# h from fp16 pairs of p and M, and packs of p turned by a transposing DMA instead of by TensorE and ScalarE

## The chip, the cores and the metric

The kernel runs on 1 core of a Trainium2 chip. The metric is the device time in microseconds of one execution. TensorE (PE), VectorE (DVE), ScalarE (ACT), GpSimd (POOL) and SyncE (SP, which issues the transfers here) run side by side and meet at semaphores.

## What is computed

Four batches of 12608 query rows with 128 channels go through an attention over 49 agents; the result goes through a feed-forward layer of 1024 hidden units with a soft gate and a layer norm. Cut to what matters:

```python
def sm(a, b):                      # a softmax of scaled products
    s = scale * (a @ b.transpose(0, 2, 1))
    e = np.exp(s - s.max(-1, keepdims=True))
    return e / (e.sum(-1, keepdims=True) + 1e-09)
agent_v = sm(agents, k) @ v        # 49 x 128 a batch
x = sm(q, agents) @ agent_v        # 12608 x 128 a batch
...
h = x @ w_in                       # 1024 columns
e = np.exp(h - h.max(-1))
solu = h * e / (e.sum(-1) + 1e-09)
ln = (solu - mean) / np.sqrt(var + 1e-06) * g_ln
out = ln @ w_out                   # back to 128 columns
```

## The kernel before

x is never formed. For each batch the kernel makes M = agent_v @ w_in (scaled by the softmax's sum), and then h = p @ M, where p is the softmax of a query over 49 agents. p stands in 128 rows as a pair: the rounded value in rows 0 to 48 and the rest in rows 64 to 112; M stands twice below itself for the same reason, and as a pair of tiles `mh` and `ml` (rounded value and rest), so h is two matmuls for each half of the 1024 columns. All four operands are fp32r, fp32 words that TensorE takes in a rounded form.

The work has three parts:

- **Phase A**, once a batch (`phase_a`): 13 chunks of keys and values, a running softmax of agents over keys, agent_v, then M. `f3` is the product with w_in, `f4h` writes `mh` on ACT, `f4l` writes `ml` on DVE. After that `q1` to `q5` find the largest element of M, turn it into a power of two by way of one row, and spread it to all partitions in `cb`: a scale for u and two constants for the layer norm.
- **Phase B**, once for each unit of 8 tiles of 128 queries (`phase_b`): the products with agents (`b0`), the maximum, the difference, the exponent, the sum, its reciprocal (`b1` to `b3r`), and on POOL the two parts of p, written into one of two standing pack tiles of 4 query tiles each (`b4`). `b5` turns the four 128x128 blocks of a pack on PE (an fp32 transpose against the identity), and `b6` evicts them from PSUM on ACT as `pT`, of which there are `PTB` = 5 buffers.
- **The tiles**, 396 of them: `c_h` makes h in one of two PSUM tensors `ph` of two banks each; `c_max` is the negated row maximum on DVE; `c_exp` the exponent with its sum on ACT; `c_u` is u = h * e times the scale, with its sum, on DVE; `c_sq` the sum of squares on ACT. For the last product u must have its 1024 columns on the partitions. `xbar(x)` chooses how: tiles with x % PEN in PEP (1 of 4, and the last two) are turned by PE in fp32 (`c_t`) and evicted by ACT (`c_ev`), and take 8 fp32 matmuls with w_out; the others are split into an fp16 pair (`c_f0` on POOL or ACT, `c_f1` on POOL), turned by a transposing DMA from SP's queue (`c_x`), and take 24 fp16 matmuls. Both are `c_w`. `c_rstd` and `c_fin` scale the result, `c_out` stores it for 4 tiles at a time.

The order of the work on each engine is fixed when the kernel is built. The class `Plan` keeps a clock for each engine; each operation has a cost, a due time and the operations that it depends on, and the plan picks for each engine what can start soonest, by the earliest due. Four PSUM banks (`px`) are handed out in the same way. The due times come from some 70 constants (`BD0` to `AEND`) that shift each kind of operation against its tile's number. What the plan says is no time of the chip: there each engine runs its list in this order and waits on semaphores.

The names that the steps touch are on lines 586 to 631 and 688 to 704 (M and its scale), 762 to 812 (p), 816 to 864 (tiles) and 985 to 1033 (what waits for what).

Of the kernel before, what the change touches and what calls it, by code (L numbers as in the profile page):

```python
# [9 lines left out]
F32 = mybir.dt.float32  # L10
# [125 lines left out]
def kernel(  # L136
# [15 lines left out]
    P = 128  # L152
# [9 lines left out]
    CPR = 792.07  # L162
    PEP = (1,)
    PEN = 4
# [4 lines left out]
    FBUF = 4  # L169
# [7 lines left out]
    BD0 = -86.23  # L177
    BD1 = -476.94
    BD2 = 170.01
    BD3 = -515.84  # L180
    BD4 = -91.39
    BD5 = -179.77
    DH = -885.13
    DMX = 874.48
    DEX = -1050.28
    DU_ = -614.84
    DSQ = 160.15
    DT = -700.62
    DEV = -791.75
    DLD = -174.95  # L190
    DW = -64.88
    DWF = 612.88
    DHF = 174.12
    DMXF = 238.03
    DEXF = -551.41
    DUF = -1018.36
    DSQF = 695.01
    AME = -96.53
    ANM = 44.67
    AEE = 89.07  # L200
    ATT = 88.11
    AET = -637.77
    AAC = -693.49
    DR = 253.95
    DFG = -705.01
    DF_ = -71.98
    DRP = 262.68
    DF0 = 954.83
    DF1 = -831.63
    DX = -85.44  # L210
    OUTD = -880.66
    OUTC = 693.15
# [6 lines left out]
    SHY = -127.74  # L219
    DHR = 489.74  # L220
    DHL = -776.94
    DMXR = 1618.01
    DMXL = -140.03
    DEXR = 898.58
    DEXL = -83.71
    DUR = -1207.82
    DUL = -701.04
    DSQR = -395.96
    DSQL = -416.83
    DTR = 489.84  # L230
    DTL = 1240.02
    DEVR = -656.35
    DEVL = 605.88
    DLDR = 445.47
    DLDL = 347.94
    DWR = -351.47
    DWL = 192.65
    ASP = 0.85
    MZ = 276.64
    ASTART = 110.74  # L240
    AEND = -395.53
# [86 lines left out]
    def load_out():  # L328
        nc.sync.dma_start(out=g_sb, in_=g_ln)
        for h in range(2):  # L330
            wd = words["out", h] = mpool.tile([P, HW, 2], I32, tag="mh" if h == 0 else "ml", name=f"wd_out{h}")
            nc.sync.dma_start(out=wd.rearrange("p (k d) t -> p k (d t)", d=C),
                              in_=wo[h * (DF // 2) : (h + 1) * (DF // 2), :].rearrange("(k p) d -> p k d", p=P))
# [86 lines left out]
    for i in range(2):  # L420
        nc.vector.tensor_tensor(out=fold[:, i, :], in0=ident[:, :AP2], in1=ident[:, AP2:], op=ALU.add)
    av_dup = const.tile([C, 2 * AP2], F32, name="av_dup")
# [12 lines left out]
    def phase_a(b, due, gate):  # L435
# [155 lines left out]
        def f4h(hf):  # L591
# [3 lines left out]
            pmm, rs, mh = ps["w", hf], res["rs"], bmats[b]["mh"]  # L595
            nc.scalar.mul(out=mh[:, sl], in_=pmm, mul=rs)

        def q1():
            res["pk"] = tiny.tile([P, 1], F32, tag="pk", bufs=2, name=f"pk{b}")
            nc.vector.tensor_reduce(out=res["pk"], in_=bmats[b]["mh"].bitcast(F32), op=ALU.max, axis=AX.X,  # L600
                                    apply_absolute_value=True)

        def q2(px):
            ps["q"] = px
            nc.tensor.transpose(px[:1, :P], res["pk"], ident)

        def q3():

            r = res["pr"] = tiny.tile([1, 2], F32, tag="pr", bufs=2, name=f"pr{b}")
            ri = r.bitcast(I32)  # L610
            nc.vector.tensor_reduce(out=r[:, 0:1], in_=ps.pop("q")[:1, :P], op=ALU.max, axis=AX.X)
            nc.vector.tensor_scalar(out=r[:, 1:2], in0=r[:, 0:1], scalar1=1e-30, scalar2=None, op0=ALU.max)
            nc.vector.tensor_scalar(out=ri[:, 0:1], in0=ri[:, 1:2], scalar1=0x7F800000, scalar2=0x7F800000,
                                    op0=ALU.bitwise_and, op1=ALU.bitwise_xor)

        def q4(px):
            ps["q"] = px
            nc.tensor.matmul(px[:, :1], ones[:1, :], res["pr"][:, :1], start=True, stop=True)

        def q5():  # L620
            cb = cbs[b] = bpool.tile([P, 3], F32, tag="cb", name=f"cb{b}")
            px = ps.pop("q")
            for i, k in enumerate((1.0, math.sqrt(1e-6 * DF) * DF, math.sqrt(1e-6 * DF) * DF * 1e-9)):
                nc.vector.tensor_scalar(out=cb[:, i : i + 1], in0=px[:, :1], scalar1=float(2.0 ** 13), scalar2=k,
                                        op0=ALU.mult, op1=ALU.mult)

        def f4l(hf):
            sl = slice(hf * HW, (hf + 1) * HW)
            pmm, rs, mh, ml = ps.pop(("w", hf)), res["rs"], bmats[b]["mh"], bmats[b]["ml"]
            nc.vector.scalar_tensor_tensor(out=ml[:, sl], in0=pmm, scalar=rs, in1=mh[:, sl].bitcast(F32),  # L630
                                           op0=ALU.mult, op1=ALU.subtract)
# [71 lines left out]
        CB[b] = op("D", q5, 0.36, at(z), [o], free=o)
# [23 lines left out]
    def phase_b(k, dues, gate=()):  # L727
# [34 lines left out]
        def b3r():  # L762
            nc.vector.reciprocal(out=r["s"], in_=r["s"])

        def b4(q):
# [5 lines left out]
            nc.gpsimd.tensor_scalar(out=pk[:, :m, :A].bitcast(F32R), in0=dv, scalar1=1.0, scalar2=0.0,  # L771
                                    op0=ALU.mult, op1=ALU.add)
            nc.gpsimd.tensor_tensor(out=pk[:, :m, AP2 : AP2 + A].bitcast(F32R), in0=dv, in1=pk[:, :m, :A],
                                    op=ALU.subtract)

        def b5(q, px):
            m = min(GT, nt - q * GT)
            r["pt", q] = px
            for j in range(m):
                nc.tensor.transpose(px[:, j * P : (j + 1) * P], packs[q][:, j, :], ident)  # L780

        def b6(q):
            m = min(GT, nt - q * GT)
            pT = pTs[b, t0 // GT + q] = bpool.tile([P, GT * P], F32R, tag="pT", bufs=PTB, name=f"pT{b}_{t0}_{q}")
            nc.scalar.copy(out=pT[:, : m * P], in_=r.pop(("pt", q))[:, : m * P])
# [15 lines left out]
        d5 = op("D", b3r, 0.12, dues[3] + 0.2, [d3])  # L801
        for q in range(nq):
# [13 lines left out]
    def c_h(x, hf):  # L816
# [3 lines left out]
        lhs = pTs[b, g][:, j * P : (j + 1) * P]  # L820
# [4 lines left out]
    def c_max(x):  # L825
        nms[x] = tiny.tile([P, 1], F32, tag="nm", name=f"nm{x}")
        nc.vector.tensor_reduce(out=nms[x], in_=phs[x], op=ALU.max, axis=AX.X, negate=True)  # L827

    def c_exp(x):
# [4 lines left out]
        nc.scalar.activation(out=es[x], in_=phs[x], func=AF.Exp, bias=nms[x], accum_out=rs_[R]["S"][:, j : j + 1])  # L834
# [4 lines left out]
    def c_u(x):  # L839
        us[x] = (epool.tile([P, DF], F32, tag="u", bufs=UBUF, name=f"u{x}"), tiny.tile([P, 1], F32, tag="su", name=f"su{x}"))  # L840
        u, su = us[x]
        nc.vector.scalar_tensor_tensor(out=u, in0=phs[x], scalar=cbs[seq[x][0]][:, :1], in1=es[x],  # L842
# [142 lines left out]
    for x in range(n):  # L985
# [7 lines left out]
        for hf in range(2):  # L993
            H[x, hf] = op("P", F(c_h, x, hf), 0.468, at(x, DH + (0.0 if xbar(x) else DHF), DHR, DHL) + 0.02 * hf,
                          [pT_op[b, t // GT], U.get(x - 2)] + mdone[b][: hf + 1], kind=0)
        grp_h[b, t // GT] = last_h[b] = H[x, 1]
        MX[x] = op("D", F(c_max, x), 1.14, at(x, DMX + (0.0 if xbar(x) else DMXF), DMXR, DMXL), [H[x, 0], H[x, 1]])
        EX[x] = op("A", F(c_exp, x), 1.115, at(x, DEX + (0.0 if xbar(x) else DEXF), DEXR, DEXL), [MX[x], U.get(x - 2), FIN.get((x // RT - 4) * RT // GT + RT // GT - 1)] + (cout if x < 2 else []), after=[EX.get(x - 1)])
        used = [T.get((x - UBUF, 0)), T.get((x - UBUF, 1)), SQ.get(x - UBUF), F1.get(x - UBUF)]
        U[x] = op("D", F(c_u, x), 1.215, at(x, DU_ + (0.0 if xbar(x) else DUF), DUR, DUL), [EX[x], CB[b]] + used, after=[U.get(x - 1)])  # L1000
        SQ[x] = op("A", F(c_sq, x), 1.185, at(x, DSQ + (0.0 if xbar(x) else DSQF), DSQR, DSQL), [U[x]] + ([om] if not x else []))
        if xbar(x):
# [3 lines left out]
                       [U[x], old] + ([] if old else wready if (len(fl) + 2) % FBUF == 2 else cin + cout),  # L1006
# [100 lines left out]
```

## Time and profile before

| what | value |
|---|---|
| median of 3 runs | 1341.16 us (1340.59 to 1342.35) |
| the profiled execution | 1340.84 us, of which the span of its instructions is 1339.1 |
| mean granted TensorE clock | 0.997 |
| DMA | 262.66 MB in 653547 packets, mean 196 GB/s |
| transposing DMAs of xt | 295, of 16 blocks of 128x128 each |

The span runs from the first to the last instruction. An engine's busy time is the union of its instructions' durations. Matmuls overlap in the pipeline, so what one costs is read from the start of one to the start of the next, and the same holds on DVE, where an instruction starts before the one ahead has ended. "Idle before, releaser" names what ended the idle time. In the groups, L823 is the line of h, L827 the row maximum, L842 u, L834 the exponent, L863 the squares, L891 the last product, L870 the transposes of u on PE, L875 their eviction, L780 and L785 those of p, L853 and L850 the fp16 parts of u on POOL, L857 the transposing DMA.

### The profile page before, as it was taken

The page shows a single profiled execution, that of the slowest core. Times are in us where ns is not written, and L with a number is a line of the kernel's source. Part 1 is how long each engine was busy: PE and PEld are TensorE (multiplying, and loading weights), DVE is VectorE, ACT ScalarE, POOL GpSimd, SP SyncE. Part 2 cuts the span into 40 slices and gives each one's busy share as a digit, 9 for nine tenths or more (in the row PEclk, how much of TensorE's full clock was granted, in tenths as well). Part 3 has the DMA queues.
Part 4 walks back from the last instruction along what each step waited for, and adds up shares of the span by engine and source line. Part 5 has one row for each costly group of instructions (what it writes and reads, how often), then busy time and mean ns, then how long its engine had stood idle before and what let it go on. Part 6 is the DMA issues. An engine that isn't in the chain of part 4 may idle for free.

```text
span 1339.1 us, 36596 instructions
## 1 busy us (share of the span) xinstructions
PE 1310.8 (98%) x14406; PEld 1127.5 (84%) x14406; DVE 1208.5 (90%) x1807; ACT 1223.3 (91%) x2258; POOL 1166.7 (87%) x1160
## 2 busy tenths in 40 slices
PE   8889999999999999999999999999899999999998
PEld 4568888888998888888888888988788888988988
DVE  6898899999998899999999999998889899999885
ACT  3489899899999999999999999999898999999996
POOL 2569899899998999998899999997689999999995
PEclk9989999999999999999999999999999999999999
DMA  9569999989989999999999999999789999987987
GB/s 363 216 153 200 247 216 238 199 171 193 177 159 223 216 190 237 218 237 191 188 186 180 212 224 197 191 239 177 155 153 186 179 182 185 170 171 143 178 165 139
DMA packets 653547, 262.66 MB, mean 196 GB/s; under 512 B 618560, under 2 KB 622144, under 8 KB 653376
## 3 DMA queue, kind: packets, MB, share of 16 engines
q1 hardware_dynamic: 653376, 260.34, 94.1%
q8 instruction: 113, 1.85, 0.6%
q14 instruction: 58, 0.48, 0.1%
HBM read 79.67 MB, written 25.95 MB: 79 GB/s over the span
## 4 chain that ended last, share of the span: by engine, by line
PE 79%; ACT 7%; DVE 6%; POOL 3%; DMA 3%; issue 2%; SPq 0%; ACTq 0%; DVEq 0%; POOLq 0%
PE px L891 37%; PE ph L823 24%; PE px L870 6%; PE px L740 3%; PE px L780 3%; ACT e L834 2%; PE px L476 2%; ACT sq L863 2%; PE px L525 2%; DMA xt<-f 2%; DVE u L842 1%; POOL f L853 1%; PE px L509 1%; DVE nm L827 1%; ACT ut L875 1%
## 5 line engine op out<-in xcount | busy, mean ns | idle before, releaser
L853 POOL TENSOR_TENSOR f<-u,f 128x1024 f16<-128x1024 f32 x295 | 631.1, 2144 | 38.2 <-ACT f L848 16.7
L842 DVE SCALAR_TENSOR_TENSOR u<-ph,cb,e 128x1024 f32<-128x1024 f32 x396 | 500.0, 1280 | 40.1 <-ACT e L834 34.5
L827 DVE TENSOR_REDUCE nm<-ph 128x1 f32<-128x1024 f32 x396 | 477.4, 1217 | 45.8 <-PE ph L823 40.4
L863 ACT ACTIVATE sq<-u,su 128x1024 bf16<-128x1024 f32 x396 | 457.4, 1155 | 23.3 <-DVE u L842 18.4
L834 ACT ACTIVATE e<-ph,nm 128x1024 f32<-128x1024 f32 x396 | 439.5, 1112 | 24.2 <-DVE nm L827 21.4
L891 PEld LDWEIGHTS <-xt 128*128 128x128 f16 x7080 | 404.7, 98 | 47.5 <-issue 43.3
L891 PE MATMUL px<-wh,xt 128*128 128x128 f16 x4720 | 441.2, 220 | 1.5 <-DMA xt<-f 1.5
L891 PE MATMUL px<-wl,xt 128*128 128x128 f16 x2360 | 409.3, 219 | 0.0
L823 PE MATMUL ph<-mh,pT 128*128 128x512 f32 x792 | 344.2, 435 | 4.5 <-DVE u L842 4.5
L823 PE MATMUL ph<-ml,pT 128*128 128x512 f32 x792 | 312.8, 395 | 0.0
L850 POOL TENSOR_SCALAR f<-u 128x1024 f16<-128x1024 f32 x234 | 244.5, 1045 | 33.2 <-DVE u L842 20.1
L891 PE MATMUL px<-w,ut 128*128 128x128 f32 x1616 | 215.9, 278 | 0.6 <-DVE ob L935 0.6
L891 PEld LDWEIGHTS px<-w,ut 128*128 128x128 f32 x1616 | 197.8, 192 | 10.9 <-issue 6.8
L823 PEld LDWEIGHTS ph<-mh,pT 128*128 128x128 f32 x792 | 150.0, 189 | 37.7 <-DVE u L842 11.3
L823 PEld LDWEIGHTS ph<-ml,pT 128*128 128x128 f32 x792 | 150.7, 190 | 19.5 <-issue 0.7
L875 ACT COPY ut<-px 128x512 f32<-128x512 f32 x202 | 114.4, 582 | 6.6 <-PE px L870 6.5
L870 PE MATMUL px<-ident,u 128*128 128x128 f32 x808 | 110.5, 274 | 0.0
L870 PEld LDWEIGHTS px<-ident,u 128*128 128x128 f32 x808 | 95.3, 142 | 13.4 <-ACT ek L502 0.2
L914 POOL TENSOR_TENSOR y<-t,nhalf 128x8 f32<-128x8 f32 (+1 forms) x50 | 81.4, 1628 | 3.8
L935 DVE TENSOR_TENSOR ob<-px,yc 128x512 f32<-128x512 f32 (+1 forms) x100 | 68.0, 680 | 13.7 <-PE px L891 9.3
L834 ACT ACTIVATION_READ_ACCUMULATOR e<-ph,nm 128x1 f32 x396 | 79.1, 200 | 0.0
L863 ACT ACTIVATION_READ_ACCUMULATOR sq<-u,su 128x1 f32 x396 | 77.5, 196 | 0.0
(133 smaller groups left out, 1219.4 us busy)
## 6 DMA issues: line engine op xcount, KB each, us to landing
out_dram<-ob SPq DMA_DIRECT2D x98, 256.0 KB, 3.0
qt<-in_qT_dram SPq DMA_DIRECT2D x48, 512.0 KB, 4.8
kt<-in_kT_dram SPq DMA_DIRECT2D x36, 512.0 KB, 4.8
vt<-in_v_dram SPq DMA_DIRECT2D x36, 512.0 KB, 5.1
kh<-in_kT_dram SPq DMA_DIRECT2D x12, 512.0 KB, 9.9
vh<-in_v_dram SPq DMA_DIRECT2D x12, 512.0 KB, 10.0
xt<-f SPq DMA_TRANSPOSE x295, 4.8
wd_in<-in_w_in_dram SPq DMA_DIRECT2D x2, 512.0 KB, 6.1
```

Of the source, the lines that this page charges most:

```text
L823: nc.tensor.matmul(ph[:, sl], lhs, bmats[b]["mh" if m == 0 else "ml"][:, sl], start=(m == 0), stop=(m == 1))
L827: nc.vector.tensor_reduce(out=nms[x], in_=phs[x], op=ALU.max, axis=AX.X, negate=True)
L834: nc.scalar.activation(out=es[x], in_=phs[x], func=AF.Exp, bias=nms[x], accum_out=rs_[R]["S"][:, j : j + 1])
L842: nc.vector.scalar_tensor_tensor(out=u, in0=phs[x], scalar=cbs[seq[x][0]][:, :1], in1=es[x], op0=ALU.mult, op1=ALU.mult, accum_out=su)
L850: nc.gpsimd.tensor_scalar(out=f[:, 0, :], in0=us[x][0], scalar1=1.0, scalar2=0.0, op0=ALU.mult, op1=ALU.add)
L853: nc.gpsimd.tensor_tensor(out=fs[x][:, 1, :], in0=us[x][0], in1=fs[x][:, 0, :], op=ALU.subtract)
L863: nc.scalar.activation(out=sq, in_=u, func=AF.Square, bias=su, scale=-float(DF), accum_out=rs_[R]["Q"][:, j : j + 1])
L870: nc.tensor.transpose(pt[:, kf * P : (kf + 1) * P], us[x][0][:, k0 * P : (k0 + 1) * P], ident)
L875: (nc.scalar.copy if k == "A" else nc.vector.tensor_copy)(out=pr[x][:, 4 * hf : 4 * hf + 4, :], in_=rr[x, hf].rearrange("p (k t) -> p k t" ...
L891: nc.tensor.matmul(po, ut, wt[:, kf, :], start=(q == 0), stop=(q == len(mm) - 1))
L914: gp.tensor_tensor(out=g("y"), in0=g("t"), in1=nhalf[:, :m], op=ALU.pow)
L935: nc.vector.tensor_tensor(out=obs[G][:, j0:j1], in0=st[G]["po"].rearrange("p (j d) -> p j d", d=C)[:, j0:j1], in1=rs_[G * GT // RT]["yc"][ ...
```

## The change

- p is scaled by 2^10 and written as an fp16 pair; M is scaled by a power of two, found from its own size, and written as an fp16 pair. So h comes out scaled, and every reader of `ph` undoes that: the row maximum becomes a minimum of h times a negative scale from `cb`, with an accumulator and a tile `junk` that nobody reads; exp gets a scale from `cb` beside its bias; u needs its scale no longer.
- The scale of M must therefore be known before M is written: `q1` (now over the two halves in PSUM), `q1m`, `q2` to `q6` stand between the product and `f4h`, and the row maximum waits for `CB` where u did.
- The pack of p is turned by a transposing DMA from SBUF on SP's queue straight into `pT`; the transposes on PE, their PSUM bank and the eviction on ACT go.
- 3 of 10 tiles go over PE, in place of 1 of 4.
- `FBUF` is 5 in place of 4, the words of w_out are loaded into `fpool`, some costs of the plan and all its due times are new.

The core of the diff (due times and costs of the plan left out):

```diff
-    PEP = (1,)
-    PEN = 4
+    PS = 10
+    PEP = (1, 4, 7)
+    PEN = 10
-    FBUF = 4
+    FBUF = 5
...
-        pk = const.tile([P, GT, P], F32, name=f"pack{i}")
+        pk = const.tile([P, GT, P], F16, name=f"pack{i}")
...
+        def q1(hf):
+            if hf == 0:
+                res["pk"] = tiny.tile([P, 2], F32, tag="pk", bufs=2, name=f"pk{b}")
+            nc.vector.tensor_reduce(out=res["pk"][:, hf : hf + 1], in_=ps["w", hf], op=ALU.max, axis=AX.X,
+                                    apply_absolute_value=True)
+        def q1m():
+            nc.vector.tensor_scalar(out=res["pk"], in0=res["pk"], scalar1=res["rs"], scalar2=None, op0=ALU.mult)
...
-                bmats[b] = {m: mpool.tile([P, DF], F32R, tag=m, name=f"{m}{b}") for m in ("mh", "ml")}
+                bmats[b] = {m: mpool.tile([P, DF], F16, tag=m, name=f"{m}{b}") for m in ("mh", "ml")}
...
-            nc.scalar.mul(out=mh[:, sl], in_=pmm, mul=rs)
+            nc.scalar.mul(out=bmats[b]["mh"][:, sl], in_=ps["w", hf], mul=cbs[b][:, 0:1])
...
             nc.vector.reciprocal(out=r["s"], in_=r["s"])
+            nc.vector.tensor_scalar(out=r["s"], in0=r["s"], scalar1=float(2.0 ** PS), scalar2=None, op0=ALU.mult)
...
-        def b5(q, px):
-            for j in range(m):
-                nc.tensor.transpose(px[:, j * P : (j + 1) * P], packs[q][:, j, :], ident)
-        def b6(q):
-            nc.scalar.copy(out=pT[:, : m * P], in_=r.pop(("pt", q))[:, : m * P])
+        def b5(q):
+            pT = pTs[b, t0 // GT + q] = bpool.tile([P, GT, P], F16, tag="pT", bufs=PTB, name=f"pT{b}_{t0}_{q}")
+            nc.sync.dma_start_transpose(out=pT[:, :m, :], in_=packs[q][:, :m, :].rearrange("p j a -> p (j a)"))
...
-        nc.vector.tensor_reduce(out=nms[x], in_=phs[x], op=ALU.max, axis=AX.X, negate=True)
+        nc.vector.tensor_scalar(out=junk, in0=phs[x], scalar1=cbs[seq[x][0]][:, 3:4], scalar2=None, op0=ALU.mult, op1=ALU.min,
+                                accum_out=nms[x])
...
-        nc.scalar.activation(out=es[x], in_=phs[x], func=AF.Exp, bias=nms[x], accum_out=rs_[R]["S"][:, j : j + 1])
+        nc.scalar.activation(out=es[x], in_=phs[x], func=AF.Exp, bias=nms[x], scale=cbs[seq[x][0]][:, 4:5], accum_out=rs_[R]["S"][:, j : j + 1])
...
-        nc.vector.scalar_tensor_tensor(out=u, in0=phs[x], scalar=cbs[seq[x][0]][:, :1], in1=es[x],
+        nc.vector.scalar_tensor_tensor(out=u, in0=phs[x], scalar=1.0, in1=es[x],
                                        op0=ALU.mult, op1=ALU.mult, accum_out=su)
...
-        MX[x] = op("D", F(c_max, x), ..., [H[x, 0], H[x, 1]])
+        MX[x] = op("D", F(c_max, x), ..., [H[x, 0], H[x, 1], CB[b]])
-        U[x] = op("D", F(c_u, x), ..., [EX[x], CB[b]] + used, after=[U.get(x - 1)])
+        U[x] = op("D", F(c_u, x), ..., [EX[x]] + used, after=[U.get(x - 1)])
```

More of the change, by code (lines that the diff above doesn't have):

```diff
@@ L175 @@
     WC = 4
[L177 to L212, printed above, removed]
+    BD0 = 513.34
+    BD1 = -77.12
+    BD2 = 94.62
+    BD3 = -717.88
+    BD4 = -309.91
+    BD5 = 228.66
+    DH = -1256.09
+    DMX = 581.29
+    DEX = -1973.58
+    DU_ = -1008.76
+    DSQ = -72.06
+    DT = -1102.95
+    DEV = -976.43
+    DLD = -427.49
+    DW = -195.51
+    DWF = 855.88
+    DHF = -429.63
+    DMXF = 612.41
+    DEXF = 162.23
+    DUF = -718.92
+    DSQF = 1579.43
+    AME = 387.52
+    ANM = 375.78
+    AEE = -726.91
+    ATT = -405.51
+    AET = -210.77
+    AAC = -597.68
+    DR = 328.58
+    DFG = 478.21
+    DF_ = -71.82
+    DRP = -396.35
+    DF0 = 1557.5
+    DF1 = 112.95
+    DX = -99.26
+    OUTD = 233.27
+    OUTC = 944.92
     VA = 7
@@ L330, in load_out @@
         for h in range(2):
[L331 removed]
+            wd = words["out", h] = fpool.tile([P, HW, 2], I32, tag="f", name=f"wd_out{h}")
             nc.sync.dma_start(out=wd.rearrange("p (k d) t -> p k (d t)", d=C),
@@ new lines, in q2, with q3 @@
+        def q2(px):
+            ps["q"] = px
+            for i in range(2):
+                nc.tensor.transpose(px[:1, i * P : (i + 1) * P], res["pk"][:, i : i + 1], ident)
+        def q3():
+            r = res["pr"] = tiny.tile([1, 4], F32, tag="pr", bufs=2, name=f"pr{b}")
+            ri = r.bitcast(I32)
+            nc.vector.tensor_reduce(out=r[:, 3:4], in_=ps.pop("q")[:1, : 2 * P], op=ALU.max, axis=AX.X)
+            nc.vector.tensor_scalar(out=r[:, 2:3], in0=r[:, 3:4], scalar1=1e-30, scalar2=None, op0=ALU.max)
+            nc.vector.tensor_scalar(out=ri[:, 1:2], in0=ri[:, 2:3], scalar1=0x7F800000, scalar2=None, op0=ALU.bitwise_and)
+            nc.vector.tensor_scalar(out=ri[:, 0:1], in0=ri[:, 1:2], scalar1=0x7F800000, scalar2=None, op0=ALU.bitwise_xor)
@@ new lines, in q4, with q5, q6 @@
+        def q4(px):
+            ps["q"] = px
+            nc.tensor.matmul(px[:, :2], ones[:1, :], res["pr"][:, :2], start=True, stop=True)
+        def q5():
+            cb = cbs[b] = bpool.tile([P, 5], F32, tag="cb", name=f"cb{b}")
+            px = ps["q"]
+            nc.vector.tensor_scalar(out=cb[:, 0:1], in0=px[:, 0:1], scalar1=res["rs"], scalar2=float(2.0 ** (13 - PS)),
+                                    op0=ALU.mult, op1=ALU.mult)
+        def q6():
+            cb, px = cbs[b], ps.pop("q")
+            for i, j, k in ((1, 0, math.sqrt(1e-6 * DF) * DF), (2, 0, math.sqrt(1e-6 * DF) * DF * 1e-9)):
+                nc.vector.tensor_scalar(out=cb[:, i : i + 1], in0=px[:, j : j + 1], scalar1=float(2.0 ** 13), scalar2=k,
+                                        op0=ALU.mult, op1=ALU.mult)
+            for i, k in ((3, -(2.0 ** -14)), (4, 2.0 ** -14)):
+                nc.vector.tensor_scalar(out=cb[:, i : i + 1], in0=px[:, 1:2], scalar1=k, scalar2=None, op0=ALU.mult)
@@ L603, in q2 @@
[L603 to L625, printed above, removed]
+            nc.scalar.mul(out=bmats[b]["mh"][:, sl], in_=ps["w", hf], mul=cbs[b][:, 0:1])
```

107 lines of the change are left out of this document (51 added, 56 removed).

## The prediction

> **What bounds the kernel now.** I read the page's first part, then the chain that ended last, the busy time by stage, the waits, and for prices the timeline of one stretch and the groups of instructions.
>
> ```profile
> span 1339.1 us, 36596 instructions
> PE 1310.8 (98%) x14406; PEld 1127.5 (84%) x14406; DVE 1208.5 (90%) x1807; ACT 1223.3 (91%) x2258; POOL 1166.7 (87%) x1160
> ```
>
> The chain, by engine and by line:
>
> ```profile
> PE 79%; ACT 7%; DVE 6%; POOL 3%; DMA 3%; issue 2%; SPq 0%; ACTq 0%; DVEq 0%; POOLq 0%
> PE px L891 37%; PE ph L823 24%; PE px L870 6%; PE px L740 3%; PE px L780 3%; ACT e L834 2%; PE px L476 2%; ACT sq L863 2%; PE px L525 2%; DMA xt<-f 2%; DVE u L842 1%; POOL f L853 1%; PE px L509 1%; DVE nm L827 1%; ACT ut L875 1%
> ```
>
> TensorE is the bound: 79% of the chain. The next view has, for three stages, the length and then the busy time (and count) of PE, weight loads, DVE, ACT and POOL.
>
> ```profile
> 0.00:100.00 100.00, 84.16 (x774) 55.68 (x775) 81.35 (x172) 53.03 (x113) 48.30 (x64) 0.97 0.74 243
> 100.00:1250.00 1150.00, 1141.74 (x12708) 994.92 (x12707) 1059.03 (x1548) 1094.64 (x2014) 1045.54 (x1031) 1.00 0.97 195
> 1250.00:1339.00 89.00, 84.90 (x928) 76.90 (x927) 68.15 (x89) 75.61 (x133) 72.91 (x67) 1.00 0.86 159
> ```
>
> (The last three columns are the granted clock, the DMA share, which counts a packet's waiting too, and GB/s.) In the middle 1150 us PE holds 99.3%, but ACT already 95.2%, DVE 92.1%, POOL 90.9%. So a gain on PE is worth its full size only until the next engine is full. DVE's longest waits are for PE's h and for ACT's exponent:
>
> ```profile
> DVE nm L827 <- PE ph L823: 40.4, 99, 1.5
> DVE u L842 <- ACT e L834: 34.5, 77, 2.8
> ```
>
> **The change, term by term.** First PE, from starts of neighbouring matmuls (start, duration, line), since their durations overlap.
>
> ```profile
> 500.62 0.22 PE L891 MATMUL px<-wh,xt 128*128 128x128 f16 x1
> 500.65 0.48 PE L823 MATMUL ph<-mh,pT 128*128 128x512 f32 x1
> 500.97 0.39 PE L823 MATMUL ph<-ml,pT 128*128 128x512 f32 x1
> ...
> 505.29 0.39 PE L823 MATMUL ph<-ml,pT 128*128 128x512 f32 x1
> ...
> 506.92 1.04 PE L870 MATMUL px<-ident,u 128*128 128x128 f32 x8
> 507.79 0.61 PE L891 MATMUL px<-w,ut 128*128 128x128 f32 x4
> 508.24 0.22 PE L891 MATMUL px<-wh,xt 128*128 128x128 f16 x1
> ...
> 508.46 0.22 PE L891 MATMUL px<-wl,xt 128*128 128x128 f16 x1
> ```
>
> 1. *h in fp16.* Seven h matmuls run from 505.29 to 506.92: 0.233 us each. Four fp16 ones of 128 columns take 0.22 us (508.24 to 508.46, the second to fourth left out). So 512 columns in fp16 cost between 0.22 and 0.233 (no faster than now). I take 0.22, the row of the same type: 4 x 396 x 0.013 = 21 us off, 0 at worst. Going from an fp16 run into h, the first h matmul takes 0.32 (500.65 to 500.97) and the fp16 one before it 0.03 instead of 0.055: 0.06 us that fp16 h should not have. At one such entry for every second or third tile (an estimate from this stretch) that is 9 us (0 to 12). The Trainium skill (TensorE: Matmul & The Clock Gate, Back-to-back issue gap) gives N / 2.4 + 2.5 ns, so 216 ns here; the trace's 128-column step agrees, no row has 512 columns in fp16, and by 216 ns the 21 us would be 27.
>
> 2. *Packs of p not turned on PE.* Eight fp32 transposes take 0.87 us (506.92 to 507.79), 0.109 each. 396 go: 43 us off.
>
> 3. *Tiles.* 1 of 4 over PE becomes 3 of 10: 295 tiles over the DMA become 276, so 19 more go over PE. Each adds 8 x 0.109 of transposes and 8 x 0.1125 (507.79 to 508.24, four) and drops 24 x 0.055: 1.77 - 1.32 = 0.45 us, 9 us on.
>
> PE in all: -21 - 9 - 43 + 9 = -64 us (-35 without any gain in h). One execution took 1340.84 us here, 1.7 over its span and 0.3 under the median 1341.16. PE alone would allow 1340.8 - 64 = 1277.
>
> Now the others.
>
> ```profile
> L780 PE MATMUL px<-ident,pack 128*128 128x128 f32 x396 | 59.7, 275 | 3.6 <-ACT ut L875 3.4
> L785 ACT CAST pT<-px 128x512 fp32r<-128x512 f32 x96 | 55.4, 581 | 3.6 <-PE px L780 3.6
> ...
> L875 ACT COPY ut<-px 128x512 f32<-128x512 f32 x202 | 114.4, 582 | 6.6 <-PE px L870 6.5
> ...
> L853 POOL TENSOR_TENSOR f<-u,f 128x1024 f16<-128x1024 f32 x295 | 631.1, 2144 | 38.2 <-ACT f L848 16.7
> ```
>
> 4. *ACT* loses the evictions of p (55 us, and four shorter ones: some 57) and gains 38 of u (38 x 0.582 = 22). exp gets its scale from a pointer beside its bias. Nearest rows, small activations with both pointers and with the bias alone:
>
> ```profile
> L906 ACT ACTIVATE t<-S,cb 128x8 f32<-128x8 f32 x46 | 18.1, 393 | 0.0
> L556 ACT ACTIVATE facp<-nmp,gm 128x13 f32<-128x13 f32 x4 | 1.3, 323 | 0.1
> ```
>
> 393 - 323 = 70 ns at most, 28 us over 396; at least nothing. Those two apply different functions, so I take half, 14. ACT: -57 + 22 + 14 = -21 (-35 to -7). *POOL* drops 19 residues of 2.144, 41 us, and some first halves; the planner may pass it a few casts of ACT.
>
> 5. *DVE.* The row maximum becomes a scaled minimum with an accumulator and a pointer; u loses its pointer.
>
> ```profile
> 504.50 1.28 DVE L842 SCALAR_TENSOR_TENSOR u<-ph,cb,e 128x1024 f32<-128x1024 f32 x1
> 505.70 0.08 DVE L842 DVE_READ_ACCUMULATOR u<-ph,cb,e 128x1 f32 x1
> 505.70 0.69 DVE L481 TENSOR_REDUCE mxp<-px 128x1 f32<-128x512 f32 x1
> 506.31 1.22 DVE L827 TENSOR_REDUCE nm<-ph 128x1 f32<-128x1024 f32 x1
> 507.44 0.20 DVE L488 TENSOR_SCALAR nmp<-mxp,nmp 128x1 f32<-128x1 f32 x1
> ```
>
> Two groups that differ in one pointer operand (busy us, mean ns):
>
> ```profile
> L488 DVE TENSOR_SCALAR nmp<-mxp,nmp 128x1 f32<-128x1 f32 x48 | 10.0, 207 | 0.2
> ...
> L486 DVE TENSOR_SCALAR nmp<-mxp 128x1 f32<-128x1 f32 x4 | 0.6, 150 | 0.0
> ```
>
> From start to start the maximum takes 1.13, and u, with PSUM source, pointer and accumulator, 1.20; its accumulator read hides beside the next instruction (both start at 505.70). So the new minimum costs 0 to 0.07 more; I take 0.07, since u is the same kind: 28 us on. A pointer costs 207 - 150 = 57 ns, if all of that is seen from start to start: 0 to 23 us off u; I take 23. The second small instruction after the reciprocal, 52 x 0.15, adds 8. The chain that finds the scale of M (two half maxima of 0.61 for one of 1.13 and some five small ones of 0.15 to 0.2) adds about 1 us in each of four batches, 4. DVE: +28 - 23 + 8 + 4 = +17 (-11 to +40).
>
> 6. *M now waits for its scale*, and the maximum waits for that chain instead of u. In the head of the chain of waits:
>
> ```profile
> 60.05 1.09 PE px L589 x2
> ...
> 70.71 1.21 DVE u L842 x2
> ```
>
> M's product ends at 61.1, but u starts at 70.7 because the scale came late. The new order, by rows: half maximum 0.69, three steps on one row and two on PE (about 2.5 with gaps), M and its rest 1.5, h 0.9, minimum and exp 2.4: u at about 69. I count nothing; up to 4 us if other DVE work stands in between. In the later batches PE has the tiles of the batch before as cover; without it 3 x 3.5 = 10 us.
>
> 7. *SP's queue.* 100 transposes of p join it, waiting for POOL's pack. Behind such a wait stand xt's transposes, loads and stores; the last matmuls wait for xt.
>
> ```profile
> L857 SPq DMA_TRANSPOSE xt<-f x295: 1317/2403/6232, 75.3 to 1321.9; - x148
> ...
> DMA to landing us min/median/max: 4.2/4.8/9.2
> ```
>
> The stores and loads issued, and how long two of them held SP:
>
> ```profile
> out_dram<-ob SPq DMA_DIRECT2D x98, 256.0 KB, 3.0
> qt<-in_qT_dram SPq DMA_DIRECT2D x48, 512.0 KB, 4.8
> kt<-in_kT_dram SPq DMA_DIRECT2D x36, 512.0 KB, 4.8
> vt<-in_v_dram SPq DMA_DIRECT2D x36, 512.0 KB, 5.1
> ```
>
> ```profile
> 1008.65 0.99 SPq L939 DMA_DIRECT2D out_dram<-ob  x1
> ...
> 1011.52 0.34 SPq L720 DMA_DIRECT2D qt<-in_qT_dram  x1
> ```
>
> xt moves 16 blocks and holds SP 1.3 to 6.2 us, 2.4 in the median: 709 us. After: 276 x 2.4 = 663, and p's quarter size at 0.6 (0.3 to 6.2, were size no matter) another 60, so SP carries 14 us more. The landing's median is close to its least, so the queue isn't full now, and five buffers of p let it run groups ahead. I price this at nothing; uncovered it is 4.2 to 9.2 us a group. The Trainium skill (VectorE: DVE Perf Modes, Rules for kernel authors) speaks against the step: a 128x128 transpose belongs on TensorE if PSUM will do, and its table has 1309 ns by DMA. The rows disagree for a batch of blocks: 4.2 / 16 = 0.26 us each, landing included.
>
> **Sum.** DVE's middle stage becomes 1059 + 17 x 0.91 = 1075 us of work, against PE's 1142 - 64 x 0.91 = 1084. So PE and DVE are nearly level, PE the fuller by 9 us, each leaning on the other through two h buffers, with ACT at 1075 behind unless casts move to POOL. Level engines won't all reach PE's present 99.3%; today's second engine holds 95.2%. I take 97% for DVE, between the two: 1075 / 0.97 = 1108, in which PE's 1084 are 98%. With head and tail of 100 + 89 and 1.7 outside the span: **1299 us**.
>
> **Rivals.**
> - *PE stays the bound and DVE follows without stalls* (minimum costs no more than the maximum did): the full 64 us, 1277; for it, PE reaches 99.3% beside an ACT at 95%. Chance 0.21.
> - *fp16 h is no faster than now* and the mode entries stay: PE gives 35 us, 1306, and with stalls of 10 us 1316. For it: no row has the shape. Chance 0.14.
> - *Slower: DVE becomes the bound and stays as full as today.* h, minimum, exp and u of a tile follow each other on two buffers, with a longer minimum in the loop; if DVE keeps 92.1% there and has its upper cost, (1059 + 36) / 0.921 = 1189, so 1380. It decides from a share of 1075 / 1150 = 93.5% down. Against it: 75 of DVE's idle us are waits for PE and for ACT, which both get lighter. Chance 0.10.
> - *The queue becomes the bound.* Each p transposed holds SP h us: 663 + the 218 stores and loads quoted, at 0.34 to 0.99 and so about 0.65 (142) + 100 h. At the median 2.4 that is 1045 and hidden; at the longest 6.2, 1425. It passes 1341 from h = 5.4. By the skill's 1309 ns a block (VectorE: DVE Perf Modes, The three transpose paths) h would be 4 x 1.309 = 5.2 and the queue's work 1329. The trace's 0.26 us a block speaks against that. Chance 0.05.
>
> **Numbers.** Forecast case 0.50, rivals 0.21, 0.14, 0.10 and 0.05. Differences within 0.2% (2.7 us) can't be told from none. The first three cases are faster: 0.85, and 0.01 of the queue, 0.86; same 0.03; slower 0.11. The range runs from the first rival, less 3 for mode entries at 12 us and 2 for a head in which u starts at 69, 1272, to the third case with DVE's upper cost, 1075 + 21 at 97%, 1130 + 191 and 10 us of stalls: 1331.
>
> **What would show it.** Right: no L780 and L785 groups; h steps of 0.22; DVE's share in the middle near 97%, PE's near 98%; nm's group near 1280 ns with an accumulator read, u's near 1220; few waits for pT. Wrong: PE still at 99% (first rival); h steps of 0.233 (second); DVE at 93% with longer waits for ph or e (third); weight loads of h, or matmuls on xt, waiting for a DMA (fourth).

## The result, and the profile after

The changed kernel takes 1485.14 us (median of 4 runs, 1483.28 to 1486.94), the kernel before beside it 1341.76 (4 runs, 1340.59 to 1344.23). The ratio is 1.1066, with a 95% interval of 1.1042 to 1.109: 143 us slower, where 1299 us had been forecast with a range of 1272 to 1331.

The page's first part for the changed kernel, busy time and share of the span by engine:

```profile
span 1484.7 us, 36533 instructions
PE 1322.9 (89%) x14049; PEld 1028.4 (69%) x14049; DVE 1265.1 (85%) x2275; ACT 1240.9 (84%) x2201; POOL 1096.3 (74%) x1117
```

No engine is full. Beside the page of before, every share has fallen: PE from 98 to 89%, ACT from 91 to 84, POOL from 87 to 74. The chain that ended last is followed back only to 758 us of the span; its line by engine:

```profile
ACT 13%; DVE 12%; POOL 8%; PE 7%; issue 5%; DMA 3%; SPq 0%; DVEq 0%; POOLq 0%; ACTq 0%
```

These shares are of the whole span and sum to 48%. Of the first half the chain says nothing, and in the second no engine leads. So the waits have to be read. Five rows of the view of waits (engine and tile, what ended the wait, us in total, times, longest; "issue" means that the view names nothing that ended it):

```profile
POOL pack L788 <- DMA pT<-pack: 227.8, 54, 9.3
PEld L833 <- issue: 126.3, 181, 6.7
PE ph L833 <- DVE u L853: 77.4, 64, 6.6
ACT e L845 <- DVE junk L837: 66.7, 67, 7.2
...
DVE logits L768 <- POOL pack L790: 43.7, 14, 6.2
```

The longest is new. Before POOL writes p into a pack, it waits for the DMA that still has to read the same tile's last content: 54 times, 4.2 us on average. Before the change the same wait was for PE's transposes, and cost next to nothing; the row in the waits of before:

```profile
POOL pack L771 <- PE px L780: 5.4, 11, 1.3
```

One such wait in the changed kernel, from the timelines of SP and POOL put in order of time (start, duration; on SP the duration is how long the transfer held the engine):

```profile
491.13 0.55 POOL L790 TENSOR_TENSOR pack<-logits,pack 128x196 f16<-128x196 f32 x1
...
507.68 7.71 SPq L868 DMA_TRANSPOSE xt<-f  x3
514.06 4.22 POOL L864 TENSOR_TENSOR f<-u,f 128x1024 f16<-128x1024 f32 x2
515.49 0.53 SPq L950 DMA_DIRECT2D out_dram<-ob  x1
516.22 3.31 SPq L868 DMA_TRANSPOSE xt<-f  x1
518.23 0.52 POOL L786 TENSOR_TENSOR logits<-logits,sm 128x196 f32<-128x196 f32 x1
519.62 0.53 SPq L458 DMA_DIRECT2D kt<-in_kT_dram  x1
520.24 1.20 SPq L796 DMA_TRANSPOSE pT<-pack  x1
524.95 0.36 POOL L788 TENSOR_SCALAR pack<-logits 128x196 f16<-128x196 f32 x1 [6.20 <-DMA pT<-pack]
```

The pack of line 491.13 is turned by the DMA of 520.24. That DMA has its place in SP's list behind the four xt transposes, the store and the load that are shown, and SP starts it as soon as the load ahead is off. The xt transposes in turn wait for POOL's `f`: that of 516.22 starts when the first of the two residues of 514.06 is done (2.11 us each, so at 516.17). POOL works until 518.75, comes to the next pack for the same tile, and stands still for 6.20 us until the DMA has landed. Everything behind on POOL stands too, the next `f` among it, and with it the next xt. So the two lists take turns in holding each other up.

Over all 100 packs, the DMA is issued 20.9 us after the write of its pack has ended, and has landed after 24.4 (medians, from the trace). With 1.0 for the write, a round through a pack takes 25.4 us. Packs are written 13.4 us apart, so two of them leave 26.8. Before the change the turn on PE started as late, 21.0 us after the write, but was over 0.6 us later: a round of 22.6 out of 26.4. So hardly anything is left to spare now, and in 54 rounds it isn't enough.

How long these transfers take (hold of SP in ns, min/median/max; then issue to landing in us), from the view of the tile `pT`:

```profile
L796 SPq DMA_TRANSPOSE pT<-pack x100: 1190/1218/2471, 41.2 to 1425.6; - x100
...
DMA to landing us min/median/max: 2.3/3.2/8.3
```

By stage (length, busy PE, weight loads, DVE, ACT, POOL, granted clock, DMA share, GB/s):

```profile
100.00:1190.00 1090.00, 961.28 (x10173) 746.97 (x10171) 922.47 (x1658) 921.16 (x1635) 798.63 (x811) 0.95 0.88 177
1190.00:1485.00 295.00, 280.00 (x3139) 230.85 (x3137) 261.59 (x437) 273.25 (x470) 253.51 (x248) 1.00 0.88 164
```

Up to 1190 us POOL is at 73% and PE at 88%, and PE's granted clock is 0.95. The last pack wait ends at 1183 (50 of the 54 lie before 970; the last load of keys and values, which share SP's queue, starts at 1044). After that all engines are fuller, and the clock is 1.00.

The groups that answer to those of before (busy us, mean ns), with instructions of different shapes kept apart:

```profile
L837 DVE TENSOR_SCALAR_CACHE_REDUCE junk<-ph,cb 128x1024 bf16<-128x1024 f32 x396 | 506.6, 1279 | 51.1 <-PE ph L833 34.9
L853 DVE SCALAR_TENSOR_TENSOR u<-ph,e 128x1024 f32<-128x1024 f32 x396 | 478.9, 1220 | 72.5 <-ACT e L845 34.9 <-POOL f L864 30.6 <-POOL t L922 2.4
L845 ACT ACTIVATE e<-ph,nm,cb 128x1024 f32<-128x1024 f32 x396 | 475.6, 1203 | 70.4 <-DVE junk L837 66.7
...
L780 DVE TENSOR_SCALAR sm<-sm 128x8 f32<-128x8 f32 x48 | 34.9, 727 | 1.6
```

The minimum (L837) and u (L853) have the lengths that the prediction gave them. The exponent has grown from 1112 to 1203 ns, and the small factor 2^10 on the sums (L780) takes 727 ns where 150 were counted.

### The profile page after: what moved, and what is told of

Same layout as the page of the kernel before. It is cut to its first block, busy times and chain, and to the rows that moved or that the text cites. A ratio compares the mean times of both kernels' runs of the same rounds, so it can differ in the third digit from the quotient of the medians.

```text
span 1484.7 us, 36533 instructions
## 1 busy us (share of the span) xinstructions
PE 1322.9 (89%) x14049; PEld 1028.4 (69%) x14049; DVE 1265.1 (85%) x2275; ACT 1240.9 (84%) x2201; POOL 1096.3 (74%) x1117
## 5 line engine op out<-in xcount | busy, mean ns | idle before, releaser
L864 POOL TENSOR_TENSOR f<-u,f 128x1024 f16<-128x1024 f32 x276 | 587.8, 2136 | 51.0 <-ACT f L859 28.8
L837 DVE TENSOR_SCALAR_CACHE_REDUCE junk<-ph,cb 128x1024 bf16<-128x1024 f32 x396 | 506.6, 1279 | 51.1 <-PE ph L833 34.9
L853 DVE SCALAR_TENSOR_TENSOR u<-ph,e 128x1024 f32<-128x1024 f32 x396 | 478.9, 1220 | 72.5 <-ACT e L845 34.9
L845 ACT ACTIVATE e<-ph,nm,cb 128x1024 f32<-128x1024 f32 x396 | 475.6, 1203 | 70.4 <-DVE junk L837 66.7
L833 PE MATMUL ph<-mh,pT 128*128 128x512 f16 x792 | 308.6, 390 | 80.3 <-DVE u L853 77.4
L833 PE MATMUL ph<-ml,pT 128*128 128x512 f16 x792 | 308.2, 389 | 0.0
L833 PEld LDWEIGHTS <-pT 128*128 128x128 f16 x1584 | 149.7, 99 | 225.6 <-issue 126.3
L902 PE MATMUL px<-w,ut 128*128 128x128 f32 x1920 | 253.7, 279 | 1.2 <-DVE ob L946 1.2
L902 PEld LDWEIGHTS px<-w,ut 128*128 128x128 f32 x1920 | 236.7, 193 | 20.9 <-issue 10.9
L845 ACT ACTIVATION_READ_ACCUMULATOR e<-ph,nm,cb 128x1 f32 x396 | 77.7, 196 | 0.0
```

Source lines behind the costliest of these rows:

```text
L833: nc.tensor.matmul(ph[:, sl], lhs, bmats[b]["mh" if m == 0 else "ml"][:, sl], start=(m == 0), stop=(m == 1))
L837: nc.vector.tensor_scalar(out=junk, in0=phs[x], scalar1=cbs[seq[x][0]][:, 3:4], scalar2=None, op0=ALU.mult, op1=ALU.min, accum_out=nms[x])
L853: nc.vector.scalar_tensor_tensor(out=u, in0=phs[x], scalar=1.0, in1=es[x], op0=ALU.mult, op1=ALU.mult, accum_out=su)
L864: nc.gpsimd.tensor_tensor(out=fs[x][:, 1, :], in0=us[x][0], in1=fs[x][:, 0, :], op=ALU.subtract)
L902: nc.tensor.matmul(po, ut, wt[:, kf, :], start=(q == 0), stop=(q == len(mm) - 1))
```

## The experiments

The theory, called A where an expectation uses letters, is that the two pack tiles form a ring through SP's queue: POOL may not write a pack until the DMA has read it, and that DMA stands behind other transfers. Against it stand the other costs: the dearer instructions on DVE and ACT, the share of tiles over PE, and the order that the planner found with its due times. Two kinds of experiment must be kept apart. Some keep the order on every engine (e1, e5, e6, e12 to e16) and change the buffers, or alter, move or leave out one kind of instruction. The others alter something that the planner reads, and it then makes another order on all engines.

Times are single executions where no interval is given. The kernel before took 1341.5 to 1344.2 us beside them.

**Four packs in place of two** (e1), same order:

```diff
-    for i in range(2):
+    for i in range(4):
...
-            pk, dv = packs[q], r["d"][:, sl, :]
+            pk, dv = packs[q + 2 * (k % 2)], r["d"][:, sl, :]
...
-            nc.sync.dma_start_transpose(out=pT[:, :m, :], in_=packs[q][:, :m, :].rearrange("p j a -> p (j a)"))
+            nc.sync.dma_start_transpose(out=pT[:, :m, :], in_=packs[q + 2 * (k % 2)][:, :m, :].rearrange("p j a -> p (j a)"))
```

> Theory A (pack ring): in the changed kernel POOL waits 228 us in 54 waits, before it writes a pack, for the transposing DMA of the pack that stood in the same of the two buffers, and all that is behind it on POOL (fp16 parts of u, so xt, so the last product) is late. With four pack buffers in place of two and the same order on every engine these waits fall under 20 us and the time to 1300 to 1360. Rival B (SP's queue): the DMAs of p take SP's time and delay xt whatever POOL does: 1460 to 1490. Rival C (the new costs on DVE and ACT): 1460 to 1490, with exp and minimum as the longest waits.

Measured: 1372.49, so 112.7 us of the 143 go, with no place in a list changed (two more packs are cleared at the start). The waits for the pack are gone, as theory A expected; the time is 12 us above its range of 1300 to 1360, so something else costs time too. Rivals B and C, at 1460 or more, fall as the main cause. From its view of waits, and its stage from 100 to 650 us, which has the full clock:

```profile
PEld L833 <- issue: 83.3, 152, 2.9
POOL f L864 <- ACT f L859: 78.1, 48, 4.7
POOL t L922 <- ACT sq L874: 53.0, 25, 4.4
...
POOL pack L788 <- DMA pT<-pack: 4.4, 2, 2.5
```

```profile
100.00:650.00 550.00, 527.20 (x5752) 408.96 (x5750) 521.74 (x928) 522.53 (x934) 450.70 (x455) 1.00 1.01 202
```

The ring is shown, and its price in this order of repairs. The DMA of a pack is issued no sooner than before (22.1 us after the write), but POOL no longer stands for it. The lower clock of the changed kernel is gone with the stalls: from 100 to 1190 us it is 1.00 here and 0.95 there.

**The plan told what the DMA costs** (e3): a hold of 1.25 in place of 0.6, a landing 2.0 us later; two packs.

```diff
-                                             (0.6, 0, 0.7 * sc)
+                                             (1.25, 0, 0.7 * sc, 2.0)
```

> The plan's price for a DMA of p is set to what was measured (SP held 1.25 us, landing about 3.2 us after the issue, in place of 0.6 and 1.2), so that it orders POOL and SP around it; two packs stay. A: the plan moves the pack away from its DMA, waits of POOL for it fall to under half, 1330 to 1420. B: the transfers are still behind xt, 1450 to 1500. C: 1470 to 1500.

Measured: 1505.44. A prediction of A fell here: with the right price the waits did not shrink, but grew. From its view of waits:

```profile
POOL pack L788 <- DMA pT<-pack: 258.2, 61, 9.3
```

**One tile of four over PE** (e4), as before the change, with two packs: `PEP = (1,)`, `PEN = 4`.

> 1 of 4 tiles over PE, as before, all else as changed: 19 more tiles' transposes on SP and POOL. A: POOL's waits stay and POOL has more work: 1480 to 1520. B: SP has 50 us more: 1500 to 1540. If the share of tiles was at fault: under 1420.

Measured: 1618.9, above every range that was expected, with 312.6 us of pack waits. More xt transposes on SP make the ring slower, but the order is another one too, so the two aren't parted by this run.

**The factor 2^10 moved to POOL** (e5): e1 and

```diff
-            nc.vector.tensor_scalar(out=r["s"], in0=r["s"], scalar1=float(2.0 ** PS), scalar2=None, op0=ALU.mult)
...
+            sv = r["s"][:, sl]
+            nc.gpsimd.tensor_scalar(out=sv, in0=sv, scalar1=float(2.0 ** PS), scalar2=0.0, op0=ALU.mult, op1=ALU.add)
```

> Four packs as in the run before, and the factor 2^10 of the sum's reciprocal moved from DVE to POOL. Theory D (port): this small DVE instruction takes 0.8 us in the mean and up to 2.1 because it waits for something that POOL holds during its 2.1 us instructions, so it costs DVE 40 us and not 8; moved, DVE's busy time falls by 35 to 40 us and the time of 1372 by 10 to 35. Rival: it is only a late neighbour, and the time moves to the next DVE instruction: DVE's busy time falls by under 12 us, the time by under 8.

> Four packs and the factor on POOL, timed against the kernel before: ring and port theories say that the two repairs bring back about 141 us of the 143, so within 0.3% of before.

Measured: 1343.68 in the first run, and with repeats 1342.02 (11 runs, 1338.99 to 1344.77) against 1341.51 before (15 runs): a ratio of 1.0002, 95% interval 0.9991 to 1.0013. So a step of 0.1 to 0.2 us on paper cost 29 us (1372.49 to 1343.68). DVE's busy time falls by 40.0 us (1266.0 to 1226.0), as theory D had it; by the rival it would have passed to DVE's next instruction. Its group in e1, and one of its instructions from the timeline with its neighbours on DVE and the POOL instruction beside them:

```profile
L780 DVE TENSOR_SCALAR sm<-sm 128x8 f32<-128x8 f32 x48 | 39.6, 825 | 1.6
```

```profile
456.11 2.13 POOL L864 TENSOR_TENSOR f<-u,f 128x1024 f16<-128x1024 f32 x1 [0.62 <-ACT f L859]
456.57 0.20 DVE L779 RECIPROCAL sm<-sm 128x8 f32<-128x8 f32 x1
456.80 1.47 DVE L780 TENSOR_SCALAR sm<-sm 128x8 f32<-128x8 f32 x1
458.18 1.21 DVE L853 SCALAR_TENSOR_TENSOR u<-ph,e 128x1024 f32<-128x1024 f32 x1
```

The reciprocal on the same 128x8 values takes 0.20 us while POOL works, the multiplication ends at 458.27, and POOL's instruction at 458.24. Of the 52 multiplications in e1, 33 take over 0.3 us, and in the trace all 33 end 0.02 to 0.03 us after an instruction of POOL ends. The 52 reciprocals take 0.15 to 0.20 us, though 36 of them run wholly inside an instruction of POOL. By these ends the multiplication waits for something that POOL holds. The Trainium skill (SBUF — State Buffer, SBUF: two separate sides) has the rule: GpSimd and a VectorE instruction in a two-port mode exclude each other from a shared pair of SBUF ports for a whole instruction. The ends in this trace agree with it; that this multiplication runs in such a mode, no run here shows.

**The same on POOL with two packs** (e14), the change's kernel with only that move:

> The changed kernel with the factor on POOL alone, two packs. If ring and port add up: 1485 - 29 = 1456. If the port's cost was hidden behind the ring's waits: 1475 to 1490. If the port was what made the ring late: 1400 or less.

Measured: 1481.53, 3.6 us better, within the 1475 to 1490 of the second case. The two costs are not fixed sizes that add up: while POOL stands for packs (210.4 us in this run), DVE's lost time is hidden behind it. Taken in this order, the factor is worth 3.6 us and the ring 1481.53 - 1342.02 = 139.5.

**No pointers in the minimum and the exponent** (e6): e5 with `tensor_reduce(op=ALU.max, negate=True)` and an exp without `scale`, as before the change.

> As the run beside it (four packs, factor on POOL), with the row maximum and the exponent issued as in the kernel before: a maximum without scale and accumulator, an exponent without the scale pointer. It leaves out that the scale of h is undone. Theory E (dearer tile work): exp falls from 1203 to 1112 ns, ACT by 36 us, DVE's maximum by 0.07 us a tile, and the time by 20 to 40 us against the run beside it. Rival F (the order): the time is set by an order that was planned for other delays, and less work only makes longer waits: under 12 us.

Measured: 1324.36, 19.3 under the first run of e5, just short of theory E's 20 to 40 and above rival F's 12. The rows of the two groups in e6:

```profile
L838 DVE TENSOR_REDUCE nm<-ph 128x1 f32<-128x1024 f32 x396 | 474.7, 1216 | 25.6 <-PE ph L834 22.3
L845 ACT ACTIVATE e<-ph,nm 128x1024 f32<-128x1024 f32 x396 | 439.2, 1112 | 20.6 <-DVE nm L838 19.1
```

By these, the scale costs 1203 - 1112 = 91 ns on ACT, 36 us in 396 tiles, and 63 ns on DVE, 25 us. Together they are worth 19 us of time. Without them the rest of the change is 19.9 us faster than the kernel before beside it (1344.24).

**What the other edits give in orders of their own.** p in fp16 turned by PE and evicted by ACT (e2, the rest as in the change):

> The packs of p, still fp16, turned by PE and evicted by ACT as before; fp16 h and 3 of 10 tiles stay. A and B: the loss goes with the DMA; PE gets 396 transposes of about 0.06 us (24 us) and ACT 47 us back, so 1300 to 1340. C: 1430 or more.

h in fp16 alone (e7: p by PE and ACT, 1 of 4, the due times of before, the factor on POOL):

> One part alone: fp16 pairs for h, with the packs of p turned by PE in fp16 and evicted by ACT, 1 of 4 tiles over PE and the due times of the kernel before; the factor on POOL. Forecast's terms: PE loses about 27 us on h, 9 on entries and 20 on transposes of half the price, ACT gains 36 on the exponent. If the parts of PE's sum hold, PE is no bound and ACT (1223 + 36) is: 1310 to 1335. If fp16 h is worth nothing because the other engines are full: 1340 to 1370.

e5, with the planner told that there are four packs (e8: `old = B5.get((k - 2, q)) or B5.get((k - 3, q))`):

> Four packs, factor on POOL, and the plan knows of the four: it lets a pack wait for the DMA two units back and not one. Ring theory: the waits of POOL stay gone, and as the plan has fewer ties the time is 1330 to 1365. If the order that is on record was the better one: 1365 to 1400.

e5 with measured costs in the plan (e9: exp 1.2 in place of 1.13, the reciprocal's step 0.12 in place of 0.25, the pack 0.13 more), and the same with e3's price of the DMA (e10):

> As the run beside it, but the plan knows the measured price of exp (1.2 for 1.13), of the reciprocal without its second step (0.12) and of the pack with the factor (0.13 more). If wrong prices in the plan are what is left (order theory), 1300 to 1335; if the due times fit only the order on record, 1340 to 1420.

> As the run with the measured prices, and the DMA of p at 1.25 us of SP and 2 us more to landing. With four packs where the plan counts two, the ring cannot bind, so the pack's lag costs nothing: within 20 us of the run with the measured prices. If POOL's waits for p's DMA come back over 50 us, the ring binds even so.

e5 with 1 tile of 4 over PE (e11):

> 1 of 4 tiles over PE with four packs and the factor on POOL. With two packs the same step cost 134 us (1619 against 1485). Ring theory: most of that was the ring too, since each transposed tile more on SP makes p's DMA later: under 30 us against 1344. If the share itself costs it: 1420 or more.

Measured: e2 1399.86, e7 1378.96, e8 1564.68, e9 1394.10, e10 1373.87, e11 1426.41. The first three missed what was expected of them. e9 lies in its second range; e10 is 20.2 us under e9, at the edge of its 20, with 12.0 us of pack waits; e11 lies in the range for the share. e8 says most. Its plan took up the slack of the new buffers: the DMA of a pack is issued 53.7 us after the write (median), where in e5 it was 21.7, and the waits are back:

```profile
POOL pack L789 <- DMA pT<-pack: 274.1, 60, 9.5
```

So here the spare buffers helped against the late transfer only while the order didn't count on them. e9 and e10 have small changes of cost alone, and are 52 and 32 us slower than e5. An edit that makes the planner choose anew moves the time by tens of us whatever its own worth, so e2, e4, e7 and e11 price nothing smaller than that. In e11 the weight loads wait 66.6 us for xt, 49 times, against 6.5 in e5; but in e10, whose share is 3 of 10, they wait 36.3. So of its 84 us over e5, the share and the new order aren't parted.

**Is TensorE the bound?** The kernel before without the products with the rest of w_out (e12), 8 of 24 matmuls of each of 295 tiles, 295 x 8 x 0.055 = 130 us of PE; and e5 without them (e13), 276 x 8 x 0.055 = 121 us:

```diff
+            if wt is wl16:
+                continue
```

> The kernel before without the products with the rest of w_out (8 of the 24 matmuls of a tile turned by DMA are left out; the order of all else is the same): 295 x 8 x 0.055 = 130 us less for PE. The prediction's reading (PE full at 99.3%, the bound): the time falls by 60 us or more, until ACT at 95% is full. Rival reading (PE's busy share counts matmuls that overlap in the pipe, and the loop of h, minimum, exp and u sets the pace): under 25 us.

> The same left out (276 x 8 x 0.055 = 121 us of PE) of the changed kernel with four packs and the factor on POOL, which takes 1342. If PE is still its bound: 1290 or less. If the 64 us that the change took from PE already put PE out of the way: within 15 us of 1342.

Measured: 1326.63 and 1341.30. Taking 130 us from the engine with 79% of the chain bought 16 us (against 1342.75), and in e5 121 us bought less than the difference between two runs. e12's first line, its chain and two rows of its waits:

```profile
PE 1237.2 (93%) x12046; PEld 1004.5 (76%) x12046; DVE 1208.4 (91%) x1807; ACT 1220.0 (92%) x2258; POOL 1167.8 (88%) x1160
...
ACT 38%; POOL 19%; DVE 18%; PE 12%; issue 9%; DMA 4%; SPq 0%; POOLq 0%; ACTq 0%; DVEq 0%
...
PEld ph L823 <- DVE u L842: 96.6, 190, 1.9
...
PE ph L823 <- DVE u L842: 45.9, 97, 1.8
```

130 us of steps took only 74 off PE's busy time, which counts overlapping durations once. ACT and DVE have the same work as before, and the chain goes over to them. The two waits of h for u were 11.3 and 4.5 us before: PE was ahead of the loop of h, maximum, exp and u by little, and much of what it gains it spends waiting for that loop.

**Which engine is it after the repair?** e5 with the squares over half of u's columns (e15: 145 us less on ACT), and with the minimum over half of h's columns (e16: 198 us less on DVE):

```diff
-        nc.scalar.activation(out=sq, in_=u, func=AF.Square, bias=su, scale=-float(DF),
+        nc.scalar.activation(out=sq[:, :HW], in_=u[:, :HW], func=AF.Square, bias=su, scale=-float(DF),
```

```diff
-        nc.vector.tensor_scalar(out=junk, in0=phs[x], scalar1=cbs[seq[x][0]][:, 3:4], scalar2=None, op0=ALU.mult, op1=ALU.min,
+        nc.vector.tensor_scalar(out=junk[:, :HW], in0=phs[x][:, :HW], scalar1=cbs[seq[x][0]][:, 3:4], scalar2=None, op0=ALU.mult, op1=ALU.min,
```

> Four packs and the factor on POOL (1342), with the squares summed over half of u's columns: about 0.43 us of ACT a tile left out, 170 us. If ACT, at 96% of the middle, sets the pace: 1290 or less. If DVE's loop does (minimum, exp, u on two h buffers): within 20 us of 1342.

> The same kernel with the minimum taken over half the columns of h: about 0.53 us of DVE a tile left out, 210 us, and as much from the loop of each h buffer. If the loop or DVE sets the pace: 1290 or less. If ACT does: within 20 us of 1342.

Measured: 1331.73 and 1330.38, so 10.3 and 11.6 us under e5's 1342.02. e5's chain, then those of e15 and e16:

```profile
ACT 38%; DVE 23%; POOL 15%; issue 11%; PE 11%; DMA 2%; DVEq 0%; POOLq 0%; SPq 0%; ACTq 0%
```

```profile
PE 36%; DVE 26%; POOL 15%; issue 8%; ACT 8%; DMA 6%; SPq 1%; DVEq 0%; POOLq 0%; ACTq 0%
```

```profile
ACT 48%; PE 18%; POOL 11%; DVE 10%; issue 8%; DMA 4%; SPq 0%; ACTq 0%; DVEq 0%; POOLq 0%
```

Each time the chain leaves the lightened engine for the others, and 145 or 198 us of work less are worth 10 or 12; an engine that set the pace was to bring 50 or more. With e13, none of PE, ACT and DVE sets the pace alone. POOL, with 15% of e5's chain, was not lightened. The lists of the engines lean on each other (in e16 u waits 153.6 us for the exponent, where in e5 it waited 43.4), and most of a gain on one engine turns into waiting on it. What an order made for these lighter engines would reach stays open: every order that was tried with e5's work was slower.

## Why the prediction was wrong, point by point

**The step that failed is 7, SP's queue**, "I price this at nothing". It asked who reads `pT` late, and found five buffers. It did not ask who waits for the transfer at its other end: the pack that it reads is free only when it has landed, there are two packs, and the writer is POOL, in order, with `f` behind it. The fourth rival had the queue as bound, with the total of its holds (1425 us at most). In the changed kernel SP is held 1014 us of 1485 in all, p's transfers taking 1.2 us each and not the 0.6 of item 7; the queue wasn't full. What cost the time was the latency in a ring that had little to spare: the landing takes 3.2 us where the turn on PE had taken 0.6. The waits of before had a row for this ring (the 5.4 us for PE); a DMA's landing, quoted in the prediction as 4.2 to 9.2 us for xt, in the place of four transposes of 0.109 would have pointed to it. Its "uncovered it is 4.2 to 9.2 us a group" is near the 54 waits of 4.2 us by luck: it meant the readers of `pT`, and the 4.2 us are how far a round overran. Of these 228 us, 113 are the price by e1.

**The opening, "TensorE is the bound", failed too**, and would have made the forecast wrong without the ring. It rested on PE's 79% of the chain and 99.3% of the middle. Matmuls that take 0.39 us from start to end and 0.233 from start to start can fill such a union even where PE has some slack. By e12, 130 us of PE are worth 16 there, so 64 us of PE alone could hardly bring the 42 us of the forecast. The Trainium skill (Perfetto Trace Analysis, Identifying the Most-Contended Engine) warns against judging by the matmuls' busy time, and has the weight loads' busy share, with the share of peak arithmetic, looked at in its place. The former was 84% here, short of full, and e12 agrees. The warning could have been weighed, and wasn't.

**Item 5, DVE.** The minimum was to cost 28 us more and costs 506.6 - 477.4 = 29.2; u was to gain 23 and gains 500.0 - 478.9 = 21.1. Both right. The reciprocal's second step was counted as 52 x 0.15 = 8 and takes 37 us of DVE, because of POOL. An instruction of the same kind stood in the profile of before, small and from SBUF to SBUF, with a mean of 850 ns: two of the four take 0.17 us, and the other two take 1.1 and 2.0 and end 0.03 us after an instruction of POOL.

```profile
L560 DVE SCALAR_TENSOR_TENSOR lsp<-lsp,facp 128x13 f32<-128x13 f32 x4 | 3.4, 850 | 0.0
```

The second step is worth 29 us of time once the ring is gone.

**Item 4, ACT.** Bounds of 0 to 70 ns for exp's scale, 35 taken; it is 91. The two small activations that the bound came from were no bound for one of 1024 columns. ACT's busy time went from 1223.3 to 1240.9, up 18 where down 21 was forecast; exp's 36 instead of 14 make 22 of these 39, and five more casts of u some 5; where the rest lies stays open.

**Items 1 to 3** were right as prices. Three neighbouring h matmuls of the changed kernel:

```profile
1285.56 0.38 PE L833 MATMUL ph<-mh,pT 128*128 128x512 f16 x1
1285.78 0.38 PE L833 MATMUL ph<-ml,pT 128*128 128x512 f16 x1
1285.99 0.38 PE L833 MATMUL ph<-mh,pT 128*128 128x512 f16 x1
```

They are 0.215 apart (0.22 forecast), the transposes and evictions of p are gone, and 276 tiles go over the DMA. The entries are right too: from an fp16 run into h, two steps took 28 + 314 ns before and take 56 + 216 now (medians), 0.07 us less, of which 0.02 belong to h; 173 such entries make 9 us. So PE was relieved about as worked out, by 64 us, and together with all else that e6 keeps this is worth no more than 20.

**Item 6**, counted at nothing, was 2.8 us: the first u starts at 73.5 in place of 70.7.

**The sum**, read the other way: 1341.8 + 113 (the ring) + 29 (the factor) + 19 (minimum and exponent) - 20 (all the rest of the change, e6 against before) = 1483, against 1485.1 measured. These are the steps from one run to the next (changed kernel, e1, e5, e6, before), so they must close but for the spread of the kernel before; the sum orders the costs and does not prove them, and in another order the ring and the factor have other sizes. The forecast had 42 us of gain; what the change saves by itself, in the order it has, is 20, and it spends 19 of that on undoing its own scale.

## What to carry to other kernels

A transfer that takes the place of an engine's instruction has two ends: ask of its source buffer, too, how many there are, who writes the next one, and what stands behind that write on its engine; the price is issue to landing plus whatever is ahead in the queue, and it is paid where the round through the buffers has nothing to spare. Before a gain is booked on a "bound" engine whose instructions overlap, take some of its work away and see whether the time follows; here 130 us bought 16. And compare orders only with like orders: in a list that is fixed by hand or by a planner, spare buffers and lighter instructions are worth what the list leaves to them.

## What the runs showed of the hardware

- A transposing DMA of four 128x128 fp16 blocks from SBUF to SBUF held SP 1.2 us and landed after 2.3 to 8.3 us (median 3.2); the one of 16 blocks held it 1.3 to 7.0. A quarter of the size took about half the hold and two thirds of the landing (medians 1.2 against 2.3, and 3.2 against 4.9).
- An instruction of DVE on 128x8 fp32 values from SBUF to SBUF took from 0.17 to 2.1 us, all that were longer than 0.3 in e1 ending with an instruction of POOL, where the reciprocal beside it never took more than 0.20. What POOL holds is inferred from these ends; no run here looked at the port itself.
- A scale from a pointer beside the bias made an activation of 1024 columns 91 ns longer.
- The granted clock fell to 0.95 over the stretch (100 to 1190 us) in which POOL's waits kept PE waiting for short times, and was 1.00 in the same order without these waits. How much of the 113 us is the clock, and how much the waits, was not parted.
